# Dealing the last weight unevenly over partitions, and ending two engines' programs in announced jumps, in a sliding-window decode-attention kernel

## The chip, the cores and the metric

The kernel runs on one core of a Trainium2 chip. The metric is the device time of one execution in microseconds; the kernel before is given by the median of three runs. One execution was also taken with the hardware profiler. All positions below are microseconds from the start of that execution's span.

## The reference, cut to what matters

One decode step for two sequences (B = 2, one query row each, D = 448). The row is layer-normalised to `xn`; 16 query heads of 256 attend over the last 2048 positions of an 8-head cache; the result goes through `wo` (4096 x 448); a gate from a small two-layer network multiplies it, and `x` is added.

```python
xn = _layernorm(x, axis=-1)
# A: q = xn @ wq; k, v = the last W = 2048 rows of the caches, each head for two query heads
scores = jnp.einsum("bhqd,bhkd->bhqk", q, k) * (Dh ** -0.5)
p = _softmax(scores, axis=-1)
o = jnp.einsum("bhqk,bhkd->bhqd", p, v)
s = o.transpose(0, 2, 1, 3).reshape(B, Sq, Hq * Dh) @ wo
# B: h = max(xn @ w1, 0); g = silu(h @ w2)
return x + s * g
```

All inputs are bfloat16. Some 44 MB have to come from device memory: 8 MB of it each for a sequence's keys and for its values, 3.7 MB each for `wq` and `wo`.

## The kernel before, in words

**Who orders the work.** The kernel keeps one list of operations per engine (`_Prog`, L23). `op` and `dma` append to a list with the operations that have to be done first; `run` (L39) turns those into semaphore waits and emits the five lists, engine by engine, as straight code without a branch. So the order on each engine and on each DMA queue is the order in which the Python code appends.

**Loads.** All large loads are issued by SyncE (SP), on one queue, in the order in which they are needed: `wq` (L189), `w1`, `w2` (L190, L191), four units of keys (L193), four of values (`load_v`, L407; the last unit in two halves, `d_v[3]` and `d_vb`), and `wo` (L441 to L443). A unit `u` is one sequence and four of the eight cache heads: 4 MB in a buffer `kv[u]` of 128 partitions, 32 KB each. The values of a unit overwrite its keys once the score matmuls of that unit are done (`last_S[u]`), so SP waits there for TensorE. The `wo` loads go into `wqo`, which held `wq`; they wait only for the q projection (`m_q`).

**wo.** `wo_src` (L185) gives each of the 128 partitions 32 consecutive rows of `wo`. It is loaded in six parts of 16, 4, 4, 4, 2 and 2 rows for each partition (`WO_PARTS`, L104), each part on all 128 partitions.

**Compute.** VectorE (DVE) transposes the keys in place in 32 x 32 blocks (`do_turn`, L273), TensorE (PE) makes the scores (`do_S`, L279), VectorE and ScalarE the softmax (`do_max`, `do_et`), TensorE spreads the weights (`do_spread`, L308), and `do_PV` (L336) multiplies each unit's values. `do_out` (L350) scales a unit's result into `o_sb`. `do_turn_out` (L360) brings the result of one head group, for both sequences, onto the partitions that hold the matching rows of `wo`: eight matmuls with a shifted selection matrix `asel` into 64 partitions of the PSUM bank `mbk`, and a copy into 64 partitions of `at2`. It runs once for each of the two head groups, after units 2 and 3.

**The output projection.** 16 of the 32 rows of each partition are multiplied four at a time, in four column strips of TensorE, into `wbk` (`WO_TILED`, L105; L446 to L450). VectorE copies `wbk` to `wc` (L451), and two fp32 matmuls with `f8` fold the four strips together into `fbk`. The other 16 rows are multiplied straight into `fbk` by `direct` (L453), two matmuls for each row, one for each half of the 448 columns. The first matmul of each part waits for that part's load (`landed`). Then VectorE multiplies by the gate (L474) and adds `x` (L476), and SP and ScalarE store one half each (L478).

**Fillers.** `fill(n)` (L332) appends n matmuls whose result nobody reads: a 32-column stationary operand `ident` and 512 columns of bfloat16. There are 10 inside the last `do_PV`, 2 in the second `do_turn_out`, 4 ahead of the output projection and 3 single ones in it: 19.

Of the kernel before, what the change touches and what calls it, by code (L numbers as in the profile page):

```python
# [5 lines left out]
BF = mybir.dt.bfloat16  # L6
F32 = mybir.dt.float32
# [4 lines left out]
PE, DVE, ACTE, SP, POOL = "pe", "dve", "act", "sp", "pool"  # L12
# [10 lines left out]
class _Prog:  # L23

    def __init__(self, nc, es):
        self.nc, self.es = nc, es
        self.lists = {PE: [], DVE: [], ACTE: [], SP: [], POOL: []}

    def op(self, eng, fn, deps=()):
# [9 lines left out]
    def run(self):  # L39
        nc = self.nc  # L40
        n = 0
        for ops in self.lists.values():
            for o in ops:
                for d in o.deps:
                    d.needed = True
        for e, ops in self.lists.items():
            sem, count = self.es.enter_context(nc.semaphore(f"s_{e}")), 0
            for o in ops:
                if o.dma:
                    n += 1  # L50
                    o.sem, o.value = self.es.enter_context(nc.semaphore(f"d_{n}")), 16
                elif o.needed:
                    count += 1
                    o.sem, o.value = sem, count

        def emit(eng, ops):
            seen = {}
            for o in ops:
                want = {}
                for d in o.deps:  # L60
                    if d.value > want.get(id(d.sem), (None, 0))[1]:
                        want[id(d.sem)] = (d.sem, d.value)
                for key, (sem, value) in want.items():
                    if value > seen.get(key, 0):
                        eng.wait_ge(sem, value)
                        seen[key] = value
                made = o.fn(eng) if o.fn else None
                if o.needed:
                    made.then_inc(o.sem, 16 if o.dma else 1)

        for eng, e in ((nc.sync, SP), (nc.gpsimd, POOL), (nc.scalar, ACTE), (nc.vector, DVE), (nc.tensor, PE)):
            emit(eng, self.lists[e])


def bass_recurrent_scan__sliding_block_cached__dense_activation_relu__decode_kernel(
# [11 lines left out]
    B, Sq, D = A_x.shape  # L87
# [13 lines left out]
    FC = DFF // 2  # L101
    NCOL = D // 2
    ROWS = 34
    WO_PARTS = [16, 4, 4, 4, 2, 2]  # L104
    WO_TILED = 16  # L105

    es = contextlib.ExitStack()
    with es:
        pr = _Prog(nc, es)

        def named(name, shape, dt):
            return es.enter_context(nc.sbuf_tensor(name, shape, dt))
# [13 lines left out]
        g8 = named("g8", [128, 8], F32)  # L126
        gsum = named("gsum", [128, 128], F32)
        f8 = named("f8", [128, 8], F32)
        asel = named("asel", [128, 72], BF)
        x_sb = named("x_sb", [128, D], BF)  # L130
        x_c = named("x_c", [128, NCOL], BF)
        xg = named("xg", [128, 9 * 128], BF)
# [27 lines left out]
        at2 = named("at2", [128, 32 * 2], BF)  # L160
# [31 lines left out]
        for u in range(NU):  # L192
# [4 lines left out]
            out=ident[:, :], in_=ident[:, :], compare_op=ALU.not_equal, fill=1.0,  # L197
            base=0, pattern=[[-1, 128]], channel_multiplier=1), [i0])
        p_z = [pr.op(POOL, lambda e, t=t: e.memset(t[:, :], 0.0))
               for t in (asel, rm, bt, qstat, at2)][-1]  # L200
# [13 lines left out]
        def red(out, in_, axis=AX.X):  # L214
# [14 lines left out]
        v_as = pr.op(DVE, lambda e: e.tensor_copy(view(asel, 7, [[8, 8]]), f8[:, :]), [v_f8, p_z])  # L229
# [10 lines left out]
        def mm(out_ap, lhsT, rhs, start, stop=False, **kw):  # L240
            return lambda e: e.matmul(out_ap, lhsT=lhsT, rhs=rhs, start=start, stop=stop,  # L241
                                      skip_group_check=True, **kw)
# [88 lines left out]

        def fill(n):  # L332
            for _ in range(n):
                pr.op(PE, mm(sbk[0][0:32, :], ident[:, 0:32], kv[0][:, 0:512], True, True), [st["exp", 2], d_v[0]])

        def do_PV(u):  # L336
            bank, p, v = obk, pt[u], kv[u]
            deps = [d_v[u], st["pt", u], z(bank), st.get(("osb", u - 1))]
            for n in range(NT // 2):
                i = n % 4  # L340
                if u == NU - 1 and n == NT // 4:
                    fill(10)
# [15 lines left out]
                op0=ALU.mult, op1=ALU.add), [v])  # L358

        def do_turn_out(hg):  # L360
            if hg:
                fill(2)
            deps = [st["osb", 2 + hg], v_as, st["mbk"]]
            lo = 64 * hg
            for dq in range(8):
                o = pr.op(PE, mm(mbk[lo:lo + 64, 288:352], asel[:, 7 - dq:71 - dq],
                                 view(o_sb, hg * 2 * DH + 32 * dq, [[DH, B], [1, 32]]),
                                 dq == 0, dq == 7, tile_position=(0, lo)), deps)
                deps = []
            st["at"] = st["mbk"] = pr.op(DVE, lambda e: e.tensor_copy(  # L370
                view(at2, 0, [[1, B], [B, 32]], n=64, p0=lo), view(mbk, 288, [[32, B], [1, 32]], n=64, p0=lo)), [o, p_z])

        def do_H():
            deps = [st["w1"], v_xr, v_q]
# [34 lines left out]

        do_H()  # L410
        do_F()
        do_turn(0, 0, 4)
        do_S(0)
        d_v[0] = load_v(0)
# [16 lines left out]
        do_rs()  # L431
        for u in range(1, NU):
            do_pt(u)
        for u in range(NU):
            do_PV(u)
            do_out(u)
            if u >= 2:
                do_turn_out(u - 2)

        landed, j0 = {}, 0  # L440
        for n in WO_PARTS:  # L441
            landed[j0] = pr.dma(SP, wqo[:, j0 * D:(j0 + n) * D], wo_src[:, j0 * D:(j0 + n) * D], [m_q])
            j0 += n  # L443
        fill(4)
        deps = [st["at"], z(wbk)]
        for j in range(WO_TILED):  # L446
            i = j % 4
# [2 lines left out]
            deps = []  # L450
        v_wc = pr.op(DVE, lambda e: e.tensor_copy(wc[:, :], wbk[:, 0:D]), [o])  # L451

        def direct(j, deps):  # L453
            for c in range(2):
                lo = j * D + c * NCOL
                o = pr.op(PE, mm(fbk[32 * c:32 * c + B, 0:NCOL], at2[:, B * j:B * j + B], wqo[:, lo:lo + NCOL],
                                 j == WO_TILED, j == 31, tile_position=(0, 32 * c)), deps)
# [11 lines left out]
        for j in range(20, 32):  # L469
            if j in (20, 24):  # L470
                fill(1)
            m_o = direct(j, [landed.get(j)])

        v_t = pr.op(DVE, lambda e: e.tensor_tensor(  # L474
            out=tmp[0:ROWS, :], in0=fbk[0:ROWS, 0:NCOL], in1=g_sb[0:ROWS, :], op=ALU.mult), [m_o, st["g"]])
# [35 lines left out]
```

## Time and profile before

| | us |
|---|---|
| three runs | 110.39, 111.76, 110.62 |
| median | 110.62 |
| the profiled execution: its time | 110.67 |
| the profiled execution: its span, first to last instruction | 109.3 |
| TensorE busy in the span | 57.0 |
| VectorE busy in the span | 62.2 |
| the SP queue's packets, as a share of the 16 DMA engines' span | 94.7% |
| mean rate from device memory over the span | 404 GB/s |
| last part of `wo` landed | 106.75 |
| last instruction's store issued | 108.02 |

The span is 1.4 us shorter than the execution's time. The profile gives the DMA share as a mean over 16 DMA engines: 0.21 in a stretch means that three or four of the sixteen still move data. [...]

### The profile page before, as it was taken

Reading aid. Unit: us, or ns where it says so; the run is one execution under the profiler, and the core shown is the slowest. Engines: PE = TensorE matmul, PEld = TensorE weight load, DVE = VectorE, ACT = ScalarE, POOL = GpSimd, SP = SyncE. Lnnn points to the kernel's source line nnn. Section 1 sums busy time; section 2 is a strip of 40 time slices with the busy share of each in tenths; the row PEclk is TensorE's granted clock in tenths of the full one; section 3 lists DMA queues with packets and bytes.
Section 4 is the critical chain, followed back from the end, with each engine's and each line's share of the span. In section 5 each row is a group of like instructions: output and inputs, shape, how many; then the busy total and the mean of one; then the engine's idle time right before and its main releaser. Section 6 shows DMA issues by size and latency. Waiting matters only on the chain.

```text
span 109.3 us, 1081 instructions
## 1 busy us (share of the span) xinstructions
PE 57.0 (52%) x458; PEld 14.5 (13%) x458; DVE 62.2 (57%) x83; ACT 9.1 (8%) x18; POOL 2.1 (2%) x12
## 2 busy tenths in 40 slices
PE   0010559430000079929952994499339555937791
PEld 0000114100000011001100120010023122413230
DVE  2920046445099979999999999930457333004102
ACT  3970000010000000002000200020110000000000
POOL 7000000000000000000000000000000000000000
PEclk9999999985555555999995569958995999999999
DMA  6899999999999999999999999999999899999940
GB/s 168 336 452 397 408 436 501 396 455 438 444 396 455 467 408 396 455 467 408 408 458 444 408 420 467 432 420 402 467 432 420 378 444 420 444 413 410 405 187 1
DMA packets 2616, 44.17 MB, mean 404 GB/s; under 512 B 306, under 2 KB 564, under 8 KB 948
## 3 DMA queue, kind: packets, MB, share of 16 engines
q1 hardware_dynamic: 2596, 44.11, 94.7%
q8 instruction: 3, 0.05, 0.2%
q14 instruction: 1, 0.01, 0.0%
q10 hardware_dynamic: 16, 0.00, 0.0%
HBM read 44.11 MB, written 0.00 MB: 403 GB/s over the span
## 4 chain that ended last, share of the span: by engine, by line
DMA 57%; DVE 28%; PE 7%; SPq 5%; issue 1%
DMA kv<-in_A_k_cache_dram 34%; DVE kv L276 24%; DMA wqo<-in_A_wo_dram 23%; PE sbk L241 7%; SPq L35 5%; DVE q_x L305 1%; DVE rm L293 1%; DVE rm_t L295 0%; DVE bias L299 0%; DVE bt L296 0%; DVE tmp L474 0%; DVE out_sb L476 0%; PE fbk L241 0%
## 5 line engine op out<-in xcount | busy, mean ns | idle before, releaser
L241 PE MATMUL sbk<-kv,qstat 128*8 128x512 bf16 x128 | 29.9, 1086 | 23.9 <-DVE kv L276 23.9
L276 DVE STREAM_TRANSPOSE kv<-kv 128x2048 f32<-128x2048 f32 x16 | 35.6, 2276 | 4.6 <-DMA kv<-in_A_k_cache_dram 4.6
L241 PE MATMUL obk<-kv,pt 128*16 128x512 bf16 x128 | 9.3, 435 | 4.8 <-DVE xg L356 2.4
L241 PEld LDWEIGHTS sbk<-kv,qstat 128*8 128x8 bf16 x128 | 4.0, 107 | 48.4 <-DVE kv L276 30.2
L353 DVE TENSOR_SCALAR o_odd<-obk,rs 128x256 f32<-128x256 f32 x4 | 1.9, 484 | 11.6 <-PE obk L241 11.6
L300 ACT ACTIVATE e_sb<-sbk,bias 128x512 bf16<-128x512 f32 x4 | 2.7, 687 | 52.6 <-DVE bias L299 52.6
L241 PE MATMUL qbk<-wqo,xr 128*4 128x512 bf16 x28 | 3.2, 626 | 5.7 <-DMA wqo<-in_A_wq_dram 5.7
L259 DVE TENSOR_SCALAR q_x<-qbk 128x512 bf16<-128x512 f32 x1 | 0.7, 691 | 8.7 <-PE qbk L241 8.7
L293 DVE TENSOR_REDUCE rm<-sbk 128x1 f32<-128x512 f32 x4 | 2.6, 662 | 4.7 <-PE sbk L241 4.7
L241 PE MATMUL sbk<-kv,ident 128*32 128x512 bf16 x19 | 5.1, 380 | 0.0
L241 PEld LDWEIGHTS obk<-kv,pt 128*16 128x16 bf16 x128 | 3.2, 97 | 10.1 <-issue 5.8
L305 DVE STREAM_TRANSPOSE q_x<-e_sb 128x512 bf16<-128x512 bf16 x4 | 2.8, 691 | 1.7 <-ACT e_sb L300 1.7
L241 PE MATMUL mbk<-ident,xg 2*128 2x2 bf16 x7 | 0.3, 163 | 6.0 <-DVE xg L234 6.0
L322 DVE TENSOR_TENSOR pt<-spk,pmask 128x512 bf16<-128x512 f32 x4 | 2.6, 684 | 0.7 <-PE spk L241 0.7
L241 PE MATMUL qbk<-w_sb,xr 128*2 128x448 bf16 x28 | 2.8, 572 | 0.0
L241 PE MATMUL fbk<-wqo,at 128*2 128x224 bf16 x32 | 2.5, 258 | 0.4 <-DMA wqo<-in_A_wo_dram 0.4
L241 PE MATMUL spk<-q_x,perm 128*32 128x128 bf16 x16 | 0.6, 292 | 3.1 <-DVE q_x L305 3.1
L474 DVE TENSOR_TENSOR tmp<-fbk,g_sb 34x224 f32<-34x224 f32 x1 | 0.4, 383 | 3.1 <-PE fbk L241 3.1
L270 DVE CAST qstat<-mbk 32x256 bf16<-32x256 f32 x4 | 1.7, 421 | 0.7 <-PE mbk L241 0.7
L356 DVE SCALAR_TENSOR_TENSOR xg<-obk,rs,o_odd 128x256 bf16<-128x256 f32 x4 | 1.9, 484 | 0.1
L451 DVE COPY wc<-wbk 128x448 f32<-128x448 f32 x1 | 0.6, 625 | 2.4 <-PE wbk L241 2.4
L241 PEld LDWEIGHTS sbk<-kv,ident 128*32 128x32 bf16 x19 | 1.8, 97 | 1.8
(70 smaller groups left out, 33.1 us busy)
## 6 DMA issues: line engine op xcount, KB each, us to landing
kv<-in_A_k_cache_dram SPq DMA_DIRECT2D x4, 4096.0 KB, 41.3
kv<-in_A_v_cache_dram SPq DMA_DIRECT2D x3, 4096.0 KB, 22.1
kv<-in_A_v_cache_dram SPq DMA_DIRECT2D x2, 2048.0 KB, 18.0
wqo<-in_A_wq_dram SPq DMA_DIRECT2D x1, 3584.0 KB, 11.3
w_sb<-in_B_w_dram SPq DMA_DIRECT2D x2, 1568.0 KB, 16.2
wqo<-in_A_wo_dram SPq DMA_DIRECT2D x1, 1792.0 KB, 23.7
wqo<-in_A_wo_dram SPq DMA_DIRECT2D x3, 448.0 KB, 24.8
wqo<-in_A_wo_dram SPq DMA_DIRECT2D x2, 224.0 KB, 25.5
```

Of the source, the lines that this page charges most:

```text
L35: o = _Op(eng, lambda e: e.dma_start(dst, src), [d for d in deps if d is not None], True)
L241: return lambda e: e.matmul(out_ap, lhsT=lhsT, rhs=rhs, start=start, stop=stop, skip_group_check=True, **kw)
L259: v_q = pr.op(DVE, lambda e: e.tensor_scalar(out=view(q_x, 0, [[256, 8], [128, 2], [1, 32]]), in0=view(qbk, 0, [[64, 8], [1, 2], [2, 32]]) ...
L270: st["q"] = st["mbk"] = pr.op(DVE, lambda e, Q=Q: e.tensor_copy(qstat[32 * Q:32 * Q + 32, 256 * Q:256 * Q + 256], mbk[32 * Q:32 * Q + 32, ...
L276: st["turn", u] = pr.op(DVE, lambda e, n=n: e.transpose(kf[:, 2048 * n:2048 * n + 2048], kf[:, 2048 * n:2048 * n + 2048]), [d_k[u]])
L293: v = pr.op(DVE, lambda e: e.tensor_reduce(out=rm[:, 0:1], in_=sbk[u % 2][:, :], axis=AX.X, op=ALU.max), [last_S[u], p_z, st.get(("rmt", u ...
L300: st["exp", u] = pr.op(ACTE, lambda e: e.activation(e_sb[:, :], sbk[u % 2][:, :], ACT.Exp, bias=bias[:, 0:1], accum_out=ssum[:, u:u + 1]), ...
L305: st["et", u] = pr.op(DVE, lambda e: e.transpose(q_x[:, 512 * u:512 * u + 512], e_sb[:, :]), [st["exp", u], m_qt])
L322: st["pt", u] = pr.op(DVE, lambda e: e.tensor_tensor(out=view(pt[u], 0, [[8, 64], [2, 4], [1, 2]]), in0=view(spk, 128 * u, [[2, 64], [0, 4 ...
L353: v = pr.op(DVE, lambda e: e.tensor_scalar(out=o_odd[:, :], in0=obk[:, DH:2 * DH], scalar1=rs[:, 2 * u + 1:2 * u + 2], scalar2=None, op0=A ...
L356: st["osb", u] = pr.op(DVE, lambda e: e.scalar_tensor_tensor(out=o_sb[:, lo:lo + DH], in0=obk[:, 0:DH], scalar=rs[:, 2 * u:2 * u + 1], in1 ...
L451: v_wc = pr.op(DVE, lambda e: e.tensor_copy(wc[:, :], wbk[:, 0:D]), [o])
```

## The change

1. The rows of `wo` are dealt in another order (`wo_src`: partition 4q + i gets the 32 rows from row 1024 i + 32 q), and unevenly. 30 rows of each of the 128 blocks are loaded as before, one block to a partition, in parts of 16, 4, 4, 4 and 2. The last two rows of all 128 blocks go to partitions 0 to 63 alone, four rows to a partition: four loads of 32 partitions, two into `wqo` behind row 30, two into `w1_sb` (free by then). They are issued ahead of the second last part. So partitions 0 to 63 hold 34 rows and 64 to 127 hold 30.
2. `do_turn_out` makes all 128 partitions of `mbk` in one accumulation: eight matmuls for the first head group, eight more for the second, with `asel` 128 columns wide, and then one copy to `at2` and two small ones to `atx` (the operand for the extra rows) after the second group.
3. 20 rows instead of 16 go through the four strips; 10 rows and the 4 extra ones go straight into `fbk`.
4. The fillers are three instead of 19: two inside the last `do_PV`, one ahead of the output projection. They are fp32, with the 8-column `f8` as stationary operand.
5. The programs of TensorE and VectorE end in a conditional branch that is always taken (`br_eq` of a register that holds 0). It leads to a block `fin` behind a never-entered block `over`. It is announced: a hint names the branch at a point far ahead, `tell[PE]` ahead of the first `do_PV`, `tell[DVE]` ahead of the first `do_turn`. The other three engines branch to `fin` without a hint.

```diff
+        def announce(e):
+            def fn(eng):
+                zero[e] = eng.alloc_register(f"zero_{e}")
+                eng.reg_mov(zero[e], 0)
+                told[e] = eng.mark_branch_hint_location()
+            return fn
+        for e in ends:
+            o = _Op(e, announce(e), [], False)
+            self.lists[e].insert(self.tell[e], o)
...
+        for e, eng in ends.items():
+            eng.br_eq(zero[e], 0, "fin", "over").branch_hint(told[e])
+        nc.br("fin", engines=[eng.engine for eng in (nc.sync, nc.gpsimd, nc.scalar)])
+        with nc.body("over", valid_engines=[eng.engine for eng in ends.values()]):
+            for eng in ends.values():
+                eng.nop()
+                eng.br("fin")
+        nc.switch_bb("fin")
...
-    WO_PARTS = [16, 4, 4, 4, 2, 2]
-    WO_TILED = 16
+    WO_PARTS = [16, 4, 4, 4, 2]
+    WO_ALL = sum(WO_PARTS)
+    WO_EXTRA = 2
+    WO_TILED = 20
...
-        asel = named("asel", [128, 72], BF)
+        asel = named("asel", [128, 160], BF)
...
-        wo_src = A_wo.rearrange("(p j) n -> p (j n)", j=32)
+        wo_src = A_wo.rearrange("(i q j) n -> q i (j n)", i=4, q=32)
...
         def fill(n):
             for _ in range(n):
-                pr.op(PE, mm(sbk[0][0:32, :], ident[:, 0:32], kv[0][:, 0:512], True, True), [st["exp", 2], d_v[0]])
+                pr.op(PE, mm(sbk[0][0:8, :], f8[:, :], kv[0][:, 0:1024].bitcast(F32), True, True),
+                      [st["exp", 2], d_v[0], v_f8])
...
-                    fill(10)
+                    fill(2)
...
         def do_turn_out(hg):
-            if hg:
-                fill(2)
             deps = [st["osb", 2 + hg], v_as, st["mbk"]]
-            lo = 64 * hg
             for dq in range(8):
-                o = pr.op(PE, mm(mbk[lo:lo + 64, 288:352], asel[:, 7 - dq:71 - dq],
+                lo = 30 - 4 * dq - 2 * hg
+                o = pr.op(PE, mm(mbk[:, 288:352], asel[:, lo:lo + 128],
                                  view(o_sb, hg * 2 * DH + 32 * dq, [[DH, B], [1, 32]]),
-                                 dq == 0, dq == 7, tile_position=(0, lo)), deps)
+                                 hg == 0 and dq == 0, hg == 1 and dq == 7), deps)
...
+            if hg == 0:
+                return
+            st["at"] = pr.op(DVE, lambda e: e.tensor_copy(
+                view(at2, 0, [[1, B], [B, WO_ALL]]), view(mbk, 288, [[32, B], [1, WO_ALL]])), [o])
+            for x in range(2):
+                st["atx"] = st["mbk"] = pr.op(DVE, lambda e, x=x: e.tensor_copy(
+                    view(atx, x * WO_EXTRA * B, [[1, B], [B, WO_EXTRA]], n=64),
+                    view(mbk, 288 + WO_ALL, [[32, B], [1, WO_EXTRA]], n=64, p0=64 * x)), [o, p_z])
...
+            if n == WO_PARTS[-2] and j0 > WO_TILED:
+                for x in range(2):
+                    for h in range(2):
+                        q, dst = 16 * x + 8 * h, (wqo[:, WO_ALL * D:], w1_sb[:, 0:WO_EXTRA * D])[x]
+                        landed["x", x, h] = pr.dma(SP, dst[32 * h:32 * h + 32, :],
+                                                   wo_src[q:q + 8, :, WO_ALL * D:], [m_q, st["h"]])
...
-        fill(4)
+        fill(1)
...
-        for j in range(WO_TILED, 20):
-            direct(j, [landed.get(j), st["g"]])
-        fill(1)
+        for j in range(WO_TILED, 24):
+            row(j, start=j == WO_TILED)
...
+        deps = [landed["x", x, h] for x in range(2) for h in range(2)] + [st["atx"]]
+        for x, w, lo in ((0, wqo, WO_ALL), (1, w1_sb, 0)):
+            for n in range(WO_EXTRA):
+                k = B * (x * WO_EXTRA + n)
+                direct(w, lo + n, deps, atx[:, k:k + B])
+                deps = []
+        for j in range(24, WO_ALL):
+            m_o = row(j, stop=j == WO_ALL - 1)
```

More of the change, by code (lines that the diff above doesn't have):

```diff
@@ L26, in __init__ @@
         self.nc, self.es = nc, es
+        self.tell = {}
         self.lists = {PE: [], DVE: [], ACTE: [], SP: [], POOL: []}
@@ L69, in emit @@
                     made.then_inc(o.sem, 16 if o.dma else 1)
+        ends = {PE: nc.tensor, DVE: nc.vector}
+        zero, told = {}, {}
+        def announce(e):
[7 more added lines that the diff above has]
+            self.lists[e].insert(self.tell[e], o)
         for eng, e in ((nc.sync, SP), (nc.gpsimd, POOL), (nc.scalar, ACTE), (nc.vector, DVE), (nc.tensor, PE)):
             emit(eng, self.lists[e])
+        for e, eng in ends.items():
[6 more added lines that the diff above has]
+        nc.switch_bb("fin")
 def bass_recurrent_scan__sliding_block_cached__dense_activation_relu__decode_kernel(
@@ L159, in bass_recurrent_scan__sliding_block_cached__dense_activation_relu__decode_kernel @@
         o_odd = named("o_odd", [128, DH], F32)
-        at2 = named("at2", [128, 32 * 2], BF)
+        at2 = named("at2", [128, WO_ALL * 2], BF)
+        atx = named("atx", [128, 2 * WO_EXTRA * 2], BF)
         wqo = named("wqo", [128, 32 * D], BF)
@@ L199, in bass_recurrent_scan__sliding_block_cached__dense_activation_relu__decode_kernel @@
         p_z = [pr.op(POOL, lambda e, t=t: e.memset(t[:, :], 0.0))
-               for t in (asel, rm, bt, qstat, at2)][-1]
+               for t in (asel, rm, bt, qstat, atx)][-1]
         v_bn = pr.op(DVE, lambda e: e.bn_stats(st6[0:B, :], x_sb[0:B, :]), [d_x])
@@ L228, in bass_recurrent_scan__sliding_block_cached__dense_activation_relu__decode_kernel @@
             view(gsum, 0, [[8, 16], [1, 8]]), view(g8, 0, [[0, 16], [1, 8]])), [v_g8])
-        v_as = pr.op(DVE, lambda e: e.tensor_copy(view(asel, 7, [[8, 8]]), f8[:, :]), [v_f8, p_z])
+        v_as = pr.op(DVE, lambda e: e.tensor_copy(view(asel, 30, [[1, 2], [32, 4]]), view(f8, 0, [[4, 2], [1, 4]])), [v_f8, p_z])
         v_perm = pr.op(DVE, lambda e: e.tensor_copy(
@@ L360, in do_turn_out @@
         def do_turn_out(hg):
-            if hg:
-                fill(2)
             deps = [st["osb", 2 + hg], v_as, st["mbk"]]
-            lo = 64 * hg
             for dq in range(8):
-                o = pr.op(PE, mm(mbk[lo:lo + 64, 288:352], asel[:, 7 - dq:71 - dq],
+                lo = 30 - 4 * dq - 2 * hg
+                o = pr.op(PE, mm(mbk[:, 288:352], asel[:, lo:lo + 128],
                                  view(o_sb, hg * 2 * DH + 32 * dq, [[DH, B], [1, 32]]),
-                                 dq == 0, dq == 7, tile_position=(0, lo)), deps)
+                                 hg == 0 and dq == 0, hg == 1 and dq == 7), deps)
                 deps = []
-            st["at"] = st["mbk"] = pr.op(DVE, lambda e: e.tensor_copy(
-                view(at2, 0, [[1, B], [B, 32]], n=64, p0=lo), view(mbk, 288, [[32, B], [1, 32]], n=64, p0=lo)), [o, p_z])
+            if hg == 0:
[6 more added lines that the diff above has]
+                    view(mbk, 288 + WO_ALL, [[32, B], [1, WO_EXTRA]], n=64, p0=64 * x)), [o, p_z])
         def do_H():
@@ L411, in bass_recurrent_scan__sliding_block_cached__dense_activation_relu__decode_kernel @@
         do_F()
+        pr.tell[DVE] = len(pr.lists[DVE])
         do_turn(0, 0, 4)
@@ L433, in bass_recurrent_scan__sliding_block_cached__dense_activation_relu__decode_kernel @@
             do_pt(u)
+        pr.tell[PE] = len(pr.lists[PE])
         for u in range(NU):
@@ L441, in bass_recurrent_scan__sliding_block_cached__dense_activation_relu__decode_kernel @@
         for n in WO_PARTS:
-            landed[j0] = pr.dma(SP, wqo[:, j0 * D:(j0 + n) * D], wo_src[:, j0 * D:(j0 + n) * D], [m_q])
+            if n == WO_PARTS[-2] and j0 > WO_TILED:
[4 more added lines that the diff above has]
+                                                   wo_src[q:q + 8, :, WO_ALL * D:], [m_q, st["h"]])
+            landed[j0] = pr.dma(SP, wqo[:, j0 * D:(j0 + n) * D], wo_src[:, :, j0 * D:(j0 + n) * D], [m_q])
             j0 += n
-        fill(4)
+        fill(1)
         deps = [st["at"], z(wbk)]
@@ L451, in bass_recurrent_scan__sliding_block_cached__dense_activation_relu__decode_kernel, with direct, row @@
         v_wc = pr.op(DVE, lambda e: e.tensor_copy(wc[:, :], wbk[:, 0:D]), [o])
-        def direct(j, deps):
+        def direct(w, j, deps, lhsT, start=False, stop=False):
             for c in range(2):
                 lo = j * D + c * NCOL
-                o = pr.op(PE, mm(fbk[32 * c:32 * c + B, 0:NCOL], at2[:, B * j:B * j + B], wqo[:, lo:lo + NCOL],
-                                 j == WO_TILED, j == 31, tile_position=(0, 32 * c)), deps)
+                o = pr.op(PE, mm(fbk[32 * c:32 * c + B, 0:NCOL], lhsT, w[:, lo:lo + NCOL],
+                                 start, stop, tile_position=(0, 32 * c)), deps)
                 deps = []
             return o
-        for j in range(WO_TILED, 20):
-            direct(j, [landed.get(j), st["g"]])
-        fill(1)
+        def row(j, **kw):
+            return direct(wqo, j, [landed.get(j), st["g"]], at2[:, B * j:B * j + B], **kw)
+        for j in range(WO_TILED, 24):
+            row(j, start=j == WO_TILED)
         deps = [v_wc]
@@ L468, in bass_recurrent_scan__sliding_block_cached__dense_activation_relu__decode_kernel @@
             deps = []
[L469 to L472, printed above, removed]
+        deps = [landed["x", x, h] for x in range(2) for h in range(2)] + [st["atx"]]
[6 more added lines that the diff above has]
+            m_o = row(j, stop=j == WO_ALL - 1)
         v_t = pr.op(DVE, lambda e: e.tensor_tensor(
```

## The prediction, as it was put on record

> **What bounds the kernel now.** I read the page's DMA lines and the chain that ended last first, then the chain in order of time, then the last stretch in steps of 0.2 us, then the DMA queues in 5 us windows.
>
> ```profile
> q1 hardware_dynamic: 2596, 44.11, 94.7%
> q8 instruction: 3, 0.05, 0.2%
> q14 instruction: 1, 0.01, 0.0%
> DMA 57%; DVE 28%; PE 7%; SPq 5%; issue 1%
> ```
>
> The load queue has all 16 DMA engines busy for 94.7% of the span; four packets carry the engines' own programs. From the chain in order of time:
>
> ```profile
> 81.24 25.50 DMA wqo<-in_A_wo_dram
> 106.75 0.04 issue
> 106.79 0.38 PE fbk L241 x4
> 107.17 0.02 issue
> 107.19 0.40 DVE tmp L474
> 107.58 0.02 issue
> 107.61 0.38 DVE out_sb L476
> ```
>
> The end hangs on the last landing of `wo` at 106.75; behind it come four matmuls, two vector operations and the stores. So a change is worth what it does to that landing, unless it puts something behind it. The last stretch, with the DMA share ahead of the last column:
>
> ```profile
> 104.40:104.60 0.20, 0.20 (x5) 0.08 (x1) 0.00 (x0) 0.00 (x0) 0.00 (x0) 1.00 0.97 376
> 104.80:105.00 0.20, 0.20 (x8) 0.19 (x5) 0.00 (x0) 0.00 (x0) 0.00 (x0) 1.00 0.58 224
> 105.40:105.60 0.20, 0.15 (x1) 0.00 (x0) 0.00 (x0) 0.00 (x0) 0.00 (x0) 1.00 0.21 81
> 105.80:106.00 0.20, 0.20 (x8) 0.17 (x4) 0.00 (x0) 0.00 (x0) 0.00 (x0) 1.00 0.21 81
> 106.20:106.40 0.20, 0.20 (x6) 0.09 (x4) 0.00 (x0) 0.00 (x0) 0.00 (x0) 1.00 0.07 27
> ```
>
> All 16 are busy until 104.5; then 13 stop within a microsecond, and three (0.21 of 16) work on alone. That last microsecond is the waste to be had. Why three? In the 5 us windows, q8 has one packet of 16 KB in each of 25 to 30, 70 to 75 and 95 to 100. The packet records behind this view settle it: a 32 KB packet takes 1.213 us and the next starts as it ends, so the packets can be strung into 16 chains, one for each DMA engine. They end at 106.47, 106.27, 106.11, 105.49, 105.34, 105.31, 105.09, 105.07, and eight between 104.99 and 104.46. The first three are the chains that the q8 packets hit, at 74.5, 96.2 and 25.8: a q8 packet takes 0.95 us, and the data packet behind it 0.47 us more than its fellows (1.681 against 1.213), so a program fetch sets one DMA engine back by 1.41 us. The chain ending at 105.49 took q14's 8 KB at 54.8 (0.31 + 0.53 = 0.84 us). Their places fit TensorE for q8 (194, some 430 and 746 of its 916 recorded instructions done) and VectorE for q14.
>
> **The change part by part.**
>
> *Dealing.* Rows 30 and 31 of a block leave their partition. On the last engine the last 2-row part takes 0.57 us from end to end. If the upper partitions are the work of eight DMA engines, each of those ends 0.57 us earlier. The four extra loads carry 128 blocks, 16 packets for each of the eight other engines at 0.071 us, and four endings of under 0.01: 1.16 us for the 0.57 removed, so each ends 0.59 later. If the engines hit at 74.5 and 25.8 serve the upper half: 106.47 - 0.57 = 105.90. The lower half then holds at worst the latest engine that no fetch delayed: 105.34 + 0.59 = 105.93. The last packet moves from 106.47 to 105.93: **-0.54 us**. No view says which partitions an engine serves. The bounds are -0.54 and, with the latest engine in the lower half, +0.59. Two engines can be told: the two-partition loads of `x` cut into the chains that end at 104.86 and 104.53, neither of them late. They write partitions 0 to 33 only; if an engine keeps to one half, both are lower, and 6 of the 14 others are too, 8 upper. I take -0.54.
>
> [...]
>
> *SP's queue.* Nine loads for six. An issue takes 0.43 to 0.60 us, so SP is done 1.3 to 1.8 us later, at some 84.8; the loads issued late reach the DMA engines at about 103, and SP then waits 24.9 us for `out_sb`. Cost 0 under that cover; uncovered, 1.8.
>
> *Announced jumps.* They can remove the q8 packet at 96.2 (fetched 10 us ahead of the end, with all but the last 170 instructions done) and q14's: those chains would end at 104.86 and 104.65. Alone that is worth nothing, since 106.47 stays; it counts only if those engines lie in the lower half, where +0.59 would otherwise make them last. The register write and the hint stand ahead of the first `do_PV`: the nearest gap there, PE's 0.57 us wait for `rinv`, and the gap of SP's bare instructions, 0.04, bound them; later PE waits 1.68 us for the last values, which hides either. VectorE waits 3.79 us for the first keys at its mark. The jump at the end of SP is on the path: 0 to 0.1, by the 0.04 to 0.07 between its issues; I take **+0.04**.
>
> *Turning the output.* The first group's copy (0.22) goes; after the second, three copies follow the matmuls, one of 0.25 and two like the small rows of 0.17 to 0.21. `at` is there at 101.1 and `atx` at 101.5; `wo`'s first rows are used at 102.5, the extra ones after 104. Wider weight loads: 0.50 us for 16 of 128 columns against 0.33 for 8 of 64, nothing. Cost 0 under 1.4 us of cover. The larger memset of `asel` (0.16 for 72 columns) ends ahead of 4.28, where its reader starts.
>
> *TensorE's end.* Eight half-row matmuls take 0.55 and four 0.35: 0.05 each and 0.15 to drain. Rows 16 to 19 now go through the strips once their part lands (103.5); with the copy of 0.62, `wc` is ready at 104.5. The part of rows 20 to 23 is used at 104.63 now. From there: eight matmuls 0.40, the fold 0.40, eight for the extra rows 0.40, eight for rows 24 to 27 0.40: TensorE is free at 106.23. The last part lands at 106.75 - 0.54 = 106.21. Even: 0 to 0.1, I take **+0.03**. Behind the extra rows' wait stand only rows 24 to 29.
>
> *Fillers.* 19 small ones go (ten took 2.32 us). A fold pass of 224 fp32 columns has 352 ns, of which 0.19 is stream, two passes a matmul: 512 columns cost about 0.85. The two inside the last `do_PV` end at 96.1, not 96.5, and the idle time ahead of 98.2 grows from 1.7 to 2.1 us. Gaps of 0.4 to 0.7 open in the projection where single fillers stood. What that does to the clock is a rival below.
>
> Sum, against the profiled execution: 110.67 - 0.54 + 0.04 + 0.03 = 110.20. It lies 0.05 over the median, so **110.15**.
>
> **The rivals.**
>
> *The late engine is in the lower half* (slower). If the chain ending at 106.47 serves partitions 0 to 63, its end is 107.06 and the time 110.62 + 0.59 + 0.07 = 111.3. It decides from the point where a lower engine ends past 105.9 undealt. For it: nothing ties fetches to a half. Against: 8 of 14.
>
> *One of the other hit engines is in the lower half.* The one of 25.8, whose fetch stays: 106.11 + 0.59 = 106.70, 110.9. The one of 96.2, if the jump is announced and the packet comes all the same: 106.27 + 0.59 = 106.86, 111.1.
>
> *The dealing does not do what it says:* the extra loads run over all 16 engines, each keeps its bytes, and 106.47 stays: 110.7. [...]
>
> *The clock.* Grants change every 3.41 us. Half clock followed windows with TensorE busy for 1.78 (to 57.8), 1.43 (to 71.4) and 0.96 us (to 81.7), and not the one with 1.74 (to 98.7). With the new fillers that window has 0.8 + 0.5 = 1.3. A half clock from 98.7 to 102.1 costs 0 to 0.25, since the landings set the pace there; if a window falls so that 104.6 to 106.3 runs at half clock, 1.6 us of stream become 3.2, and the end moves by 1.5: 111.7. [...]
>
> **How the numbers follow.** Forecast 0.52 (its own range 109.9 to 110.4); late engine below 0.17; another hit engine below 0.15; no dealing 0.08; clock 0.08. The range reaches from 109.8 to 111.3: it leaves out the clock and the edges of the others, under 2 in 10. About 2% (2.2 us) is what a measurement of this kernel can tell from no change: faster than 108.4 needs a gain that no view offers, 0.02; slower than 112.8 a half clock through the whole projection, 0.03; within, 0.95.
>
> **What would show it.** Dealing right: in the last microsecond the share drops from 1 to 0 within 1.2 us instead of 2, and the last landing is near 106.2. Wrong: three or four engines alone at the end, past 106.5. Jumps right: two q8 packets instead of three ahead of 100, no q14 packet at 55. SP: nine issues ended by 85. TensorE even: no wait of more than 0.1 ahead of the last four matmuls, and not late. Clock: a grant of 0.50 behind 98. The prediction is wrong if the last landing moves by something other than the dealing, or if the end no longer waits for it.

## The result and the profile after

| | before | after |
|---|---|---|
| median of 20 runs each, us | 110.59 (110.31 to 111.76) | 111.34 (110.68 to 113.42) |
| the profiled execution: its time | 110.67 | 111.48 |
| its span | 109.3 | 109.3 |
| its time outside the span | 1.4 | 2.2 |
| first part of `wo` landed | 102.40 | 102.74 |
| last part of `wo` landed | 106.75 | 106.68 |

The ratio is 1.006, 95% interval 1.0039 to 1.0081: slower by 0.6%, where 0.4% faster was forecast. Within 2% it counts as the same, but the interval lies clear of 1. Ratios here and below leave out runs over 1.5% above the fastest of the same kernel (two of the twenty of after, 112.72 and 113.42), and they lie near the ratio of the means, so they can differ from the ratio of the two medians. The profiled execution is one of the short ones: the spans of the twenty runs of after go from 109.3 to 110.9, with a median of 109.75.

Three lines of the page of after, two queues of section 3 (packets, MB, share of 16 engines) and the shares of the chain that ended last:

```profile
q1 hardware_dynamic: 2612, 44.11, 95.1%
q8 instruction: 2, 0.03, 0.1%
DMA 56%; DVE 28%; PE 9%; SPq 4%; issue 1%
```

q14's line is gone and q8 has two packets for three, as announced; the load queue has 16 packets more. But its share went up, from 94.7% to 95.1% of a span of the same length, with not a byte more to load.

The chain of after in order of time (start, duration, what):

```profile
80.42 24.59 DMA wqo<-in_A_wo_dram
105.01 0.04 issue
105.06 2.04 PE fbk L267 x32
107.10 0.02 issue
107.12 0.39 DVE tmp L519
107.52 0.02 issue
107.54 0.38 DVE out_sb L521
```

It goes through rows 20 to 23 (landed 105.01) and all of TensorE's matmuls behind them. The last landing is as close: 106.68, with the same four matmuls of 0.38 and the 0.04 of issue, also ends at 107.10. TensorE and the load end together, as forecast, but both half a microsecond behind the forecast. The last stretch of after (columns as before, DMA share and GB/s last):

```profile
104.40:104.60 0.20, 0.00 (x0) 0.00 (x0) 0.20 (x1) 0.00 (x0) 0.00 (x0) 1.00 0.96 367
105.40:105.60 0.20, 0.20 (x8) 0.12 (x4) 0.00 (x0) 0.00 (x0) 0.00 (x0) 1.00 0.67 260
105.80:106.00 0.20, 0.20 (x6) 0.18 (x4) 0.00 (x0) 0.00 (x0) 0.00 (x0) 1.00 0.20 72
106.20:106.40 0.20, 0.20 (x10) 0.18 (x8) 0.00 (x0) 0.00 (x0) 0.00 (x0) 1.00 0.00 0
```

The tail is the one that dealing was to make: at 105.5 two thirds of the engines still work (0.67 for 0.21), at 106.2 none (0.00 for 0.07). What is wrong lies ahead of it. The last values landed at 98.46 (98.17 before), the first part of `wo` at 102.74 (102.40): the stream was 0.3 late before the first byte that the change moves. And the packet records say why: the median 32 KB packet of the load queue took 1.215 us, for 1.213 before, and the 14,336 B, 3,584 B and 1,792 B ones of `wo` 538, 142 and 74 ns, for 535, 140 and 74. A unit of 4 MB takes 9.71 us on an undelayed DMA engine, for 9.68; over eight such units that makes 0.24 of the 0.3.

The other new thing lies behind the span. The DMA queues of after in the window 110 to 112:

```profile
q8 instruction: 1, 0.02, 3.0%
```

The packet starts at 110.75, when the span of 109.3 is over. If it is TensorE's third fetch, which its queue suggests, then in this execution the fetch did not go away but moved behind the end.

### The profile page after: what moved, and what is told of

Read it like the earlier page. It is cut to its first block, busy times and chain, and to the rows that moved or that the text cites. A ratio compares the mean times of both kernels' runs of the same rounds, so it can differ in the third digit from the quotient of the medians.

```text
span 109.3 us, 1067 instructions
## 1 busy us (share of the span) xinstructions
PE 55.1 (50%) x445; PEld 13.4 (12%) x445; DVE 62.2 (57%) x84; ACT 9.1 (8%) x18; POOL 2.1 (2%) x12
## 3 DMA queue, kind: packets, MB, share of 16 engines
q1 hardware_dynamic: 2612, 44.11, 95.1%
## 4 chain that ended last, share of the span: by engine, by line
DMA 56%; DVE 28%; PE 9%; SPq 4%; issue 1%
DMA kv<-in_A_k_cache_dram 34%; DVE kv L302 24%; DMA wqo<-in_A_wo_dram 23%; PE sbk L267 7%; SPq L36 4%; PE fbk L267 2%; DVE q_x L331 1%; DVE rm L319 1%; DVE rm_t L321 0%; DVE bias L325 0%; DVE bt L322 0%; DVE tmp L519 0%; DVE out_sb L521 0%
## 5 line engine op out<-in xcount | busy, mean ns | idle before, releaser
L267 PE MATMUL obk<-kv,pt 128*16 128x512 bf16 x128 | 8.8, 415 | 5.5 <-DMA kv<-in_A_v_cache_dram 2.7
L267 PE MATMUL sbk<-kv,f 128*8 128x512 f32 x6 | 2.9, 592 | 0.0
L267 PE MATMUL mbk<-xg,asel 128*128 128x64 bf16 x16 | 0.8, 195 | 2.2 <-DVE xg L383 2.2
L267 PE MATMUL fbk<-wqo,at 128*2 128x224 bf16 x20 | 1.4, 258 | 0.8 <-DMA wqo<-in_A_wo_dram 0.8
L267 PE MATMUL wbk<-wqo,at 128*2 128x448 bf16 x20 | 1.3, 352 | 1.0 <-DMA wqo<-in_A_wo_dram 0.9
```

## The experiments

Each result is the median of the kernel's runs, for that of the kernel before on the same chip, with the ratio and its 95% interval (not the ratio of the medians, as said above). The theory at the start was that one part of the change costs what the others save; rivals were the fillers (clock), the jumps, the dealing on the wrong half, and, once the packets were seen to be longer, the place of the load buffers.

**The parts, one at a time** (e1 to e4).

`e1`, before with the new fillers only:

```diff
-                pr.op(PE, mm(sbk[0][0:32, :], ident[:, 0:32], kv[0][:, 0:512], True, True), ...)
+                pr.op(PE, mm(sbk[0][0:8, :], f8[:, :], kv[0][:, 0:1024].bitcast(F32), True, True), ...)
-                    fill(10)
+                    fill(2)
...
-        fill(4)
+        fill(1)
```

> The kernel before with the three fp32 fillers in place of its 19, nothing else. Theory 1 (clock: with few fillers a 3.41 us window around 95 to 101 has too little TensorE work in most executions, and the half clock that follows slows the output projection): slower by 0.4 to 1.0 us in the median, with executions spread over 1.5 us and more, and with spans that differ as the granted clock does. Theory 2 (the announced jumps cost time outside the span): within 0.1 us of before. Theory 3 (the dealing makes TensorE's last chain the bound): within 0.1 us of before.

Measured: 110.88 for 110.76, ratio 1.0012 (0.999 to 1.0034). No cost that can be told in this layout.

`e2`, before with the announced jumps only (the announcement, the two `br_eq` with their hints, the marks ahead of the first `do_turn` and `do_PV`):

> The kernel before with the announced jumps, nothing else. Theory 1: within 0.1 us of before; the fetch at 96 gone, and with it one of the three late DMA engines, but not the last one. Theory 2: slower by 0.4 to 0.8 us, with the difference between the execution's time and its span larger than 1.4 us. Theory 3: within 0.1 us.

Measured: 110.61 for 110.76, ratio 0.9987 (0.9967 to 1.0007). Its queue line and the end of its chain:

```profile
q8 instruction: 2, 0.03, 0.1%
81.72 25.08 DMA wqo<-in_A_wo_dram
106.79 0.04 issue
106.84 0.38 PE fbk L263 x4
```

The fetch of 96 is gone, and the last landing stays at 106.79 (106.75): worth nothing alone, as forecast, though not by the same engine. In before the one hit at 74.54 is the last. In e2 it is the one hit at 26.15, which lands 1.9 to 2.1 us behind the earliest in every load from there to the end, while the one hit at 75.26 is 1.3 to 1.5 behind. So which engine ends last had changed from one execution to the next without any dealing.

`e3`, the dealing only (after without jumps and with the 19 old fillers):

> The dealing, the new turn of the output and 20 rows in the strips, with 19 bf16 fillers as before (10, 2, 4, and the three single ones together ahead of row 20) and no jumps. Theory 1: faster than before by 0 to 0.4 us (the fetch of 96 may now fall on an engine of the lower half, which would end up to 0.4 us behind the old last landing: then 0 to 0.4 us slower, but with a narrow spread). Theory 2: the same as theory 1. Theory 3: slower by 0.4 us or more, with TensorE never waiting for the last landing.

Measured: 111.15 for 110.76, ratio 1.0056 (1.0028 to 1.0084): slower, so the loss comes with the dealing's edits. In its profile the last landing is 107.20. The last of the eight landings that end the first extra load is 104.64, 0.49 behind the seventh, and that engine stays last to the end; the fetch of q14 at 56.17 fits it. That is the rival "late engine in the lower half", with VectorE's fetch for TensorE's.

`e4`, after with the 19 old fillers:

> The changed kernel with bf16 fillers in the old places (10, 2, 4, and the three single ones together ahead of row 20); dealing and jumps stay. Theory 1: 110.0 to 110.4 us, faster than before by 0.2 to 0.6, and a narrow spread. Theory 2: 110.7 to 111.2. Theory 3: 111 and more.

Measured: 111.39 for 110.76, ratio 1.0057 (1.0021 to 1.0093), last landing 106.71. The new fillers are not what makes after slow, and neither is the lack of jumps in e3: what e3 and e4 share is the dealing's edits. e3 and e4 both have the longer packets of after (1.215 and 538), e1 and e2 the shorter ones of before (1.213 and 535).

**The place of the buffers** (e5, e6, e12). What makes the packets of loads longer that nobody moved? The diff makes `asel` 320 bytes for 144 and adds `atx` ahead of `wqo`, and buffers lie in the order of their declaration. In the compiled programs `wqo` and the four `kv` start at a multiple of 256 bytes of the partition before (`kv[0]` at 97,024 = 379 x 256) and 192 bytes past one after (97,216).

`e5`, before with an unused tensor of 192 bytes ahead of `wqo`, and `e12`, the same with 32 bytes:

```diff
+        pad = named("pad", [128, 96], BF)
         wqo = named("wqo", [128, 32 * D], BF)
```

> The kernel before with one unused tensor of 192 bytes a partition ahead of wqo, so that wqo, w1_sb, w2_sb and the four kv buffers start 192 bytes past a multiple of 256, as they do in the changed kernel; nothing else. Address theory (every load packet into a buffer that does not start on a multiple of 256 bytes takes some 4 ns longer, from the first load on): packets of 32 KB at 1.215 us instead of 1.213, v2 landing 0.25 to 0.3 us later against its start, the last landing 0.4 to 0.5 us later, and a time 0.35 to 0.55 us over before. Pattern theory (the new order of the rows of wo makes the last loads slower): within 0.1 us of before. TensorE theory (the chain behind rows 20 to 23): within 0.1 us.

Measured: 111.25 for 110.79, ratio 1.0066 (1.0043 to 1.0088). One declaration, nothing else, costs as much as the whole change does. (It is not the whole miss: a gain of that size was forecast, so this cost alone would have left the time where it was.) The end of its chain:

```profile
81.50 25.68 DMA wqo<-in_A_wo_dram
107.19 0.04 issue
107.23 0.38 PE fbk L242 x4
```

The last landing is 107.19 for 106.75, the packets are those of after (1.215, 538, 142), the unit of 4 MB takes 9.71.

> The kernel before with an unused tensor of 32 bytes a partition ahead of wqo: the load buffers start 32 bytes past a multiple of 256. Address theory, if any start off a multiple of 256 costs the same: packets of 32 KB at 1.215 us, the time 0.4 to 0.7 us over before, as with 192 bytes. If only the distance to 64 or 128 counts, the packets are longer still; if the cost grows with the bytes read or written beyond the line, they are between 1.213 and 1.215.

Measured: 111.5 for 110.69, ratio 1.006 (1.0032 to 1.0087), last landing 107.36, packets of 1.216, 539, 144. So 32 bytes off cost no less than 192, and the packets are even a little longer: what counts is not the distance alone. That 256 is the unit is not shown, since no run has its large buffers at 128 past a multiple. For small packets that distance cost nothing: in e14 and e16 the extra loads into `wqo` start 128 bytes past a multiple of 256 and those into `w1_sb` on one, and all their packets take the same, 41 ns in e14 (896 B) and 107 ns in e16 (2,688 B). Why a moved start costs the large packets anything no run shows; what they show is its size, 0.3% for 4 MB (9.71 against 9.68 us).

`e6`, after with an unused tensor of 64 bytes, which brings the buffers back to a multiple of 256:

```diff
+        pad = named("pad", [128, 32], BF)
         wqo = named("wqo", [128, 32 * D], BF)
```

> The changed kernel with one unused tensor of 64 bytes a partition ahead of wqo, so that the load buffers start on a multiple of 256 bytes again; nothing else. Address theory: packets of 32 KB back at 1.213 us, the last landing 0.4 to 0.5 us earlier than in the changed kernel, the time 110.1 to 110.6 us, so a ratio to before of 0.995 to 1.000. Pattern theory: no change from the changed kernel, ratio 1.006. TensorE theory: ratio 1.002 to 1.006, since the chain behind rows 20 to 23 stays the bound.

Measured: 110.99 for 110.79, ratio 1.0024 (0.9995 to 1.0053). The packets are those of before again (1.213, 535, 140), and the last landing is 106.22, where the prediction had 106.21. But the execution did not end with it. Steps of e6, the stretches between which the granted clock can change (TensorE busy first; the clock is the third figure from the end of a line), and pieces of its chain:

```profile
94.87:98.28 3.41, 1.30 (x7) 0.20 (x9) 0.00 (x0) 0.00 (x0) 0.00 (x0) 1.00 1.00 426
98.28:101.69 3.41, 2.30 (x25) 0.85 (x18) 0.97 (x2) 0.00 (x0) 0.00 (x0) 0.50 0.96 402
101.69:105.10 3.41, 3.41 (x25) 1.01 (x26) 0.45 (x3) 0.00 (x0) 0.00 (x0) 0.50 0.94 372
```

```profile
103.02 2.31 PE wbk L268 x16
105.36 0.64 DVE wc L491
106.03 1.52 PE fbk L268 x24
107.56 0.02 issue
```

TensorE was busy for 1.30 us of 94.87 to 98.28, where little but the two fp32 fillers stands, and then has half clock for two steps. It multiplies the first 20 rows at half speed, without a pause (3.41 of 3.41), `wc` comes at 106.0 instead of 104.5, and TensorE is done at 107.56, 0.9 behind the last landing and its four matmuls. In after's own profile the clock stayed at 1.00 in the whole tail. Its steps run from 94.69 to 98.10 and on from there, with TensorE busy for 1.65 us of the first; the stretches shown lie 0.1 later:

```profile
94.80:98.20 3.40, 1.54 (x4) 0.18 (x2) 0.00 (x0) 0.00 (x0) 0.00 (x0) 1.00 1.01 429
98.20:101.70 3.50, 2.08 (x26) 0.69 (x26) 1.41 (x5) 0.00 (x0) 0.00 (x0) 1.00 0.96 399
```

**The dealing in the right place** (e7, e8, and e15, the program of e7 on another chip). `e7` is e3 and `e8` is e4, each with the 64 bytes.

> The dealing alone (19 bf16 fillers, no jumps) with the load buffers on a multiple of 256 bytes. Address theory: 0.4 to 0.5 us faster than the dealing alone without it, 110.5 to 110.8, ratio 0.999 to 1.002; the fetch at 96 stays and makes some lower engine late. Pattern and TensorE theory: ratio 1.004 to 1.006.

Measured: 110.77 for 110.79, ratio 1.0023 (0.9997 to 1.005), last landing 106.52. The Address theory had 0.999 to 1.002 and the others 1.004 and more, so the ratio settles little. Six spans lie at 109.0 to 109.2 and six at 109.7 to 110.2; the kernel before on that chip had 109.1 to 109.7.

> The changed kernel with the load buffers on a multiple of 256 bytes and 19 bf16 fillers (10, 2, 4 and three single ones together ahead of row 20). Address theory: as with the three fp32 fillers, within 0.2 us; 110.0 to 110.5. If the clock matters beside it, this one is the faster by 0.2 us or more, with a narrower spread. Pattern and TensorE theory: ratio 1.004 to 1.006.

Measured: 110.47 for 110.79, ratio 1.0011 (0.998 to 1.0042); its shortest 110.18, for 110.40 of before. Two stretches of its tail and pieces of its chain:

```profile
94.80:98.20 3.40, 2.17 (x17) 0.85 (x19) 0.00 (x0) 0.00 (x0) 0.00 (x0) 1.00 1.00 428
101.70:105.10 3.40, 2.66 (x35) 1.14 (x37) 0.62 (x1) 0.00 (x0) 0.00 (x0) 1.00 0.92 365
```

```profile
83.88 21.83 DMA wqo<-in_A_wo_dram
105.70 0.04 issue
105.75 0.55 PE fbk L268 x8
106.31 0.38 PE fbk L268 x4
```

The clock is full: in e8's own steps TensorE is busy for 3.26 us (92.99 to 96.40) and 1.73 us (96.40 to 99.81). The last landing is at 106.26, and TensorE is free for it at 106.30. This one execution is the forecast as it was meant: its span is 108.9, 0.4 under that of before. But the median of twelve is not clearly faster.

`e11`, e7 without any filler:

> The aligned dealing without jumps and without a single filler. Clock theory: in most executions a half clock reaches into the projection; slower than the same kernel with 19 fillers (110.77 in the median) by 0.5 to 1.5 us, and the profile shows a grant of 0.50 between 98 and 106. If the fillers do nothing: 110.5 to 111.0.

Measured: 111.53 for 110.69, ratio 1.0056 (1.0025 to 1.0087). Its profile shows half clock from 95.27 to 105.51, in an execution with a span of 109.0; most of the others were at 110.0 to 110.7. So the median is where the clock theory put it, but the one execution that was profiled lost little by its half clock, and what made the others long was not seen. That fillers are worth something here is likely and not shown: the interval is clear of that of e15 (0.9948 to 1.0017), which is the same kernel with fillers, and not of that of e7 (0.9997 to 1.005).

**Where the gain goes** (e9, e10, e13 to e16). By "lower half" is meant from here on the eight DMA engines on which the extra loads run, by "upper half" the other eight; which partitions they serve otherwise no run shows. If the late engines are in the upper half in some executions and in the lower half in others, dealing makes the good ones shorter and the bad ones longer, and more so with each row dealt.

> As the aligned changed kernel with 19 bf16 fillers, but dealt 33 rows to 31: one row of each block is moved instead of two. Half theory (which DMA engines the two program fetches fall on changes from execution to execution; where both fall on engines of partitions 64 to 127 the dealing shortens the end, where one falls on the other half it lengthens it): two groups of executions, their spans 0.5 to 0.65 us apart instead of the 1.1 of the 34 to 30 dealing, the shorter one 0.25 us longer than there (109.1). Theory that the long executions come from something else (the clock, the start): the groups stay 1.1 us apart.

> As the aligned changed kernel with 19 bf16 fillers, but dealt evenly: 32 rows to each partition, in parts of 16, 4, 4, 4, 2 and 2; jumps, new turn of the output and 20 rows in the strips stay. Half theory: one group of executions within 0.6 us, spans 109.1 to 109.7, the time within 0.2 us of before. If the new turn and the 20 rows cost something of their own: slower than before by 0.2 us or more.

Both are e8 with another share. 33 to 31 rows: 110.89 for 110.69, ratio 1.0005 (0.9968 to 1.0041), spans 108.9 to 110.2; 32 to 32: 110.9, ratio 1.0022 (0.9994 to 1.0051), spans 109.0 to 110.1. Inconclusive: with jumps in both, the spread of the even one is as large. So the same once more on one chip, four shares, without jumps and with the old fillers:

```diff
-    WO_PARTS = [16, 4, 4, 4, 2]
+    WO_PARTS = [16, 4, 4, 4, 1]
-    WO_EXTRA = 2
+    WO_EXTRA = 3
```

(for e16; 3 and 1 for e14; e13 has `[16, 4, 4, 4, 2, 2]` and no extra loads, operands and matmuls.)

> Dealt evenly, 32 rows to 32, buffers on a multiple of 256, 19 bf16 fillers, no jumps; new turn of the output and 20 rows in the strips. Half theory (a program fetch falls on an engine of the one or the other half, from execution to execution): the spans spread no wider than those of before, and the median is within 0.2 us of before. Theory that the long executions come from somewhere else (the start, the clock, the chip): the same spread as in the three dealt kernels beside it.

> As the even one, with one row of each block moved: 33 to 31. Half theory: longest less shortest span 0.5 to 0.6 us more than with 32 to 32, the shortest 0.2 to 0.3 shorter. Other theory: the same spread as with 32 to 32.

> As the even one, with two rows moved: 34 to 30. Half theory: longest less shortest span 1.0 to 1.2 us more than with 32 to 32, two groups 1.1 apart. Other theory: the same spread as with 32 to 32.

> As the even one, with three rows moved: 35 to 29. Half theory: the long group 0.55 us longer than with 34 to 30; the short group no shorter than there, since the lower half's engines without a fetch now end last (some 0.3 us later than with 34 to 30): two groups 0.8 to 1.2 us apart, both above those of 34 to 30, the median 0.4 to 0.6 us above. Other theory: one group, 0.3 us longer than with 34 to 30.

| rows | median | ratio (95%) | spans |
|---|---|---|---|
| 32 / 32 (e13) | 110.91 | 1.0004 (0.9981 to 1.0026) | 109.1 to 109.9, evenly spread |
| 33 / 31 (e14) | 110.88 | 0.9998 (0.9963 to 1.0033) | six 108.9 to 109.2, six 109.9 to 110.3 |
| 34 / 30 (e15) | 110.43 | 0.9982 (0.9948 to 1.0017) | eight 108.8 to 109.3, one 109.6, three 110.2 to 110.7 |
| 35 / 29 (e16) | 111.47 | 1.0036 (1.0 to 1.0072) | five 109.2 to 109.4, seven 110.0 to 110.8 |

The even kernel has one group, each dealt one two, with 0.6 to 0.9 us between them. Longest less shortest span is 0.8 us for the even one and 1.4, 1.9 and 1.6 for the dealt ones: with one and two rows 0.6 and 1.1 more, as the half theory had it, with three rows less than it had, and there the median is 1.0 above that of 34 to 30 where 0.4 to 0.6 was expected. Twelve executions each are few for this: the kernel before has 109.1 to 110.3 in 35 on that chip. And e16's profile is of its longest span, 110.8. Its last stretch and pieces of its chain:

```profile
106.20:106.40 0.20, 0.00 (x0) 0.00 (x0) 0.00 (x0) 0.00 (x0) 0.00 (x0) 1.00 0.17 67
106.60:106.80 0.20, 0.00 (x0) 0.00 (x0) 0.00 (x0) 0.00 (x0) 0.00 (x0) 1.00 0.09 36
107.40:107.60 0.20, 0.20 (x8) 0.04 (x2) 0.00 (x0) 0.00 (x0) 0.00 (x0) 1.00 0.04 13
```

```profile
83.86 24.07 DMA wqo<-in_A_wo_dram
107.92 0.04 issue
107.96 0.66 PE fbk L246 x10
108.63 0.02 issue
```

At 106.3 fewer than three engines still work, at 107.5 one, and TensorE mostly waits. The fourth extra load, which only eight engines work on, ends on five of them at 104.48 to 104.85, on the others at 105.27, 106.07 and 106.83; the last of these goes on to 108.20, the last landing of all. Here the fetches hit two of the lower engines; the last of them lands its share of the last values at 98.92, behind a fetch at 96.86, and no other engine is later than 98.00. In e15's profile, with a span of 109.1, it is otherwise: the part ahead of the extra loads lands on the latest engine at 104.76, and the first extra load on the latest of its eight at 103.94, so that the late engines are not among the eight. The same comparison gives 105.01 and 103.88 in after, 104.58 and 103.71 in e6, but 105.18 and 105.59 in e16. Of all eleven profiles of dealt kernels only e16's has the extra load behind. In the others it lands 0.4 to 1.1 us ahead, so that the engines set back most are not among the eight (in e3 one of the eight, set back less, still ends last, as said above). The five with the buffers in the right place and spans of 108.9 to 109.1 (e7, e8, e11, e14, e15) are all among these ten. So the profiles of one long and of five short executions are as the half theory says. That it is behind the other long ones is inferred from the two groups, and it can't be behind every one: e6's execution is long (109.8) with its late engines in the upper half, through the clock. Nor does the theory give the sizes: by the prediction's terms the distance of the groups should grow by nearly 0.6 us with each row dealt (1.16 for two), and the gap is as wide with one row as with three.

## Why the prediction was wrong, point by point

**The step that failed** is one that the sum did not have: "The larger memset of `asel` (0.16 for 72 columns) ends ahead of 4.28, where its reader starts." The larger `asel` was costed as an instruction, at 0, and the chains of packets were taken over as they were. But it also moves everything that is declared behind it, and with `atx` the load buffers start 192 bytes past a multiple of 256. e5 shows the size by itself: +0.44 in the last landing, +0.46 in the median. No row of the trace of before shows such a load, so the cost should have been bounded, as other unseen ones were; that a declaration moves the bound resource's own buffers was not thought of. That is 0.46 of a miss of 1.2 us (110.15 forecast, 111.34 measured). The second step that failed is the -0.54 for the dealing, taken as the same in every execution where it holds in some; the rest is in the points below.

**The dealing** was right in mechanism where it could be seen: with the buffers put back the last landing is 106.22 (e6) and 106.26 (e8), for a forecast of 106.21. That it fits to a hundredth is luck. The five profiles of kernels dealt 34 to 30 with the buffers in place have 106.22 to 106.52 (e6, e7, e8, e11, e15), the five of undealt ones 106.42 to 106.86 (before, e1, e2, e10, e13); the means are 0.3 apart, not 0.54, and the five dealt ones all have their late engines in the upper half. The shortest spans fit better: 108.7 in e6 and e8, where the prediction's sum makes 108.8, and 109.3 in after, half a microsecond more, as e5 has it. Eight engines ran each extra load: its semaphore is raised once at the issue (82.25 for the first one in after) and then eight times, between 103.54 and 103.88, where that of a part on all 128 partitions is raised 16 times (100.97 to 102.74 for the first part). That eight engines would run them, on which the -0.54 rests, was the author's assumption, and so was that the upper partitions are the work of the other eight. The eight landings bear out the first and speak against the rival in which the extra loads run over all 16; the second no run shows.

**Which half is late** was taken for a fixed fact, "8 of 14", and was given a chance as such. The runs speak for something that changes from execution to execution: two groups in e14 to e16, late engines in the upper half in the profiles of after, e6 and e15, and a late lower one in those of e3 and e16. The rival with 0.17 and that with 0.15 are real, but they come beside the forecast, not instead of it, so that the median of a dealt kernel falls in either group. That is where the gain goes, as far as the runs show it.

**The jumps** did what was said inside the span. "+0.04" at the end was mis-sized. The time outside the span is 1.3 to 1.4 in every run of a kernel without jumps; in after it has a median of 1.44, is over 1.45 in seven of 20 runs, and goes up to 2.6. As a mean that is some 0.2 us (1.57 against 1.33). Why only some executions pay it is open. A late fetch may be part of it: after's profile, with 2.2 outside, has one at 110.75. But e9's has one at 108.17 with 1.4 outside, and those of e2, e4, e6, e8 and e10 have no third fetch at all, e10's with 1.7 outside.

**The clock** was seen as a rival at 111.7 with 0.08. A form of it is what e6's profile shows (+0.9 behind the last landing); e1 shows no cost in the median, and e6 against e8 (1.0024 and 1.0011, with wide intervals) does not settle one. Half clock came after a step with 1.30 us busy (e6) and not after 1.65 (after) or 1.74 (before), in the order of the prediction's rows except one of 1.78. All 18 profiles together sharpen this: from 40 us on, all 55 full-clock steps with under 1.5 us of TensorE work were followed by half clock, of those with 1.5 to 2.25 us 15 of 80, and none of the 112 with more. e16, with all 19 fillers, had half clock from 98.85 to 102.27 after a step with 0.97 us. The length of a pause alone does not tell: TensorE's pause in e6's step is 2.11 us, and one of 2.16 in after, which ends at 98.50, has full clock behind it.

**SP's queue** cost nothing, as said, but was not done by 85: the ninth issue starts at 84.73 and takes 2.48 us, to 87.20, and those of the extra loads 0.68 to 0.80 each, for the 0.43 to 0.60 of the prediction. SP then still waits 20.7 us for `out_sb`.

**Turning the output and TensorE's end** were right: `at2` and `atx` in time; 2.04 us from rows 20 to 23 to the end of TensorE's work, for 1.98 by the prediction's terms, even with the last landing. The two fp32 fillers of the last `do_PV` took 1.88 us for an estimate of 1.7. (Its 0.19 of stream is worked out from rows of before: matmuls of 224 and 512 bf16 columns have a mean of 258 and 380 ns, so some 163 ns are there for any number of columns, and a pass of 224 fp32 columns with 352 ns has 189 left.)

**The sum** by what was measured: 110.15 + 0.46 for the buffers + 0.1 to 0.2 for the time outside the span = 110.7 to 110.8. The other 0.5 to 0.6 of 111.34 is about what an execution loses where a lower engine is late, or where half clock reaches the projection. How much is the one and how much the other was not told apart in after itself. No version beat the kernel before beyond its interval; nearest is e15, the dealing in the right place alone, 0.9982 (0.9948 to 1.0017).

## What to carry to other kernels

Where the load stream is the bound, look at the addresses that a change gives its buffers: a tensor that grows ahead of them is a change to every load, and the median packet duration, unmoved loads included, is the quickest check (in e5 1.215 us for 1.213, and a last landing 0.44 us later). An imbalance seen in one execution is a thing to deal against only if it is the same in the next (the last engine was the one hit at 74.54 in before and the one hit at 26.15 in e2); look at several, or at the spread of the times, first. And an edit that removes work from the span can put it behind it: read the time outside the span too (in after up to 2.6 us, for 1.3 to 1.4).

## What the runs showed of the hardware

- A load whose buffer starts 32 or 192 bytes off a multiple of 256 in its partition (e12, e5): 32 KB packets of 1.215 to 1.216 us for 1.213, 14,336 B 538 to 539 for 535 ns, 3,584 B 142 to 144 for 140, and a last landing 0.4 to 0.6 us later on a stream of 44 MB. A start 128 bytes off cost nothing on packets of 896 and 2,688 B (e14, e16).
- A program fetch does not always set back the same DMA engines: upper ones in the profiles of after, e6 and e15, a lower one in those of e3 and e16. The first extra load's latest landing, less that of the part ahead of them, is -1.13 us in after, -0.87 in e6, -0.82 in e15 and +0.41 in e16.
- With an announced jump the fetch of 96.17 is gone from the stream (after, e2, e4, e6, e8, e9, e10). Two of these seven profiles have one at the end instead (110.75 in after, 108.17 in e9), the others none. Outside the span, executions of after take 1.36 to 2.62 us, those of kernels without jumps 1.27 to 1.40.
- Half clock can last for two steps of 3.41 us although TensorE is busy for 2.30 of the first of them (e6, 98.28 to 105.10).
- Under 1.5 us of TensorE work in a full-clock step of 3.41 us was followed by half clock each time from 40 us on (55 of 55 steps in 18 profiles), over 2.25 us never (0 of 112).
